# Reordering the first loads, touching rows ahead of them, and keeping a softmax in PSUM: a change to a fused attention and feed-forward kernel

## The chip, the cores and the metric

The kernel runs on one core of a Trainium2 chip. The metric is the device time of one execution in microseconds (us), lower is better. A quoted time is the median of several executions; a verdict needs a difference of 2%. Beside each timed execution stands the span that its profile shows; the time is 1.7 to 1.8 us longer than the span, so that spans of different kernels can be compared.

## The reference

The input `x` has 2048 rows of 512 values (bf16). It is normalized over each row; the result feeds two branches, and both are added to `x`.

```python
xn = layernorm(x)                                  # eps 1e-5, no weights
# A: 32 heads of 16; each position attends to 8 keys, at distances 0, 2, ..., 14
q, k, v = split(xn @ wqkv)                         # wqkv 512 x 1536
logits  = einsum("bhsd,bhswd->bhsw", q, kg) * 16 ** -0.5    # masked where the key would be before row 0
a = einsum("bhsw,bhswd->bhsd", softmax(logits), vg).reshape(...) @ wo
# B: gated feed-forward, 1376 wide
h = gelu(xn @ w_gate) * (xn @ w_up)
out = x + a + h @ w_down
```

## The kernel before

The program is laid out by a list scheduler inside the kernel file: every instruction is a task with an engine, an estimated duration, its reads and writes, and a priority (lower goes first); a table of shifts (`SHIFT`) moves the priorities of whole groups. The rows are worked on in four blocks of 512 (16 tiles of 128). After a short head, TensorE multiplies; the other engines evict, normalize, form the products for the attention (VectorE, the `UNI` tiles) and run the softmax. What the change and the argument touch:

```python
# loads, all on SyncE's queue, in the order of prio: x0 (two of 128 rows), Wq, x1, Wk, Wv, x2 ...
G.task("sp", "ld_x0_%d" % t2, 0, mk_ld(), wr=[(it_x, t2)], prio=-960 + t2, nbytes=128 * 1024)
XIN[:, it.slot, :, :], x2[256 * p:256 * p + 256, :].rearrange("(t q) d -> q t d", q=128))       # x1, x2, ...
G.task("sp", "ld_x%d" % p, ..., prio=(0, -899.5, -897.5, -897)[p] if p < 4 else -950 + p * 20)
Wqkv[:, :, i * 512:(i + 1) * 512], A_wqkv[:, i * 512:...].rearrange("(k p) n -> p k n", p=128)  # Wq, Wk, Wv
t_ld["w" + nm] = G.task("sp", "ld_w" + nm, 0, mk(), ..., prio=-900 + i, nbytes=512 * 1024)
# ... (cut)
# normalization of a tile: statistics, aggregate, + eps, square root on GpSimd (pow), reciprocal, (x - mean) * rstd
G.task("pool", "sq%d" % t, 0.65, ...)              # e.tensor_tensor(..., op=ALU.pow)
chain(["bnst0", "bnag0", "ve0", "bnst1", "rstd0", "norm0", "bnag1", "ve1", "sub1", "rstd1", "norm1",
       "bnst2", "bnag2", "ve2", "sub2", "bnst3", "rstd2", "norm2", "bnag3", "ve3", "sub3", "rstd3", "norm3"])
# ... (cut)
# softmax of a block: logits in two PSUM banks, differences, exponentials and sum in SBUF (tile DE)
out=dev(), in0=lgv(...), in1=msb(0), op=ALU.subtract          # d2: PSUM -> DE
e.activation(out=DE[...], in_=DE[...], func=ACTF.Exp)         # exp
e.tensor_reduce(out=msv(1), in_=devw(), axis=AX.X, op=ALU.add)# d4: sum over 8 keys
# ... (cut)
cparts = [(0, 256), (256, 512)] if t in TAIL_SPLIT else [(0, 512)]      # last two tiles of the output in halves
```

Of the kernel before, what the change touches and what calls it, by code (L numbers as in the profile page):

```python
# [16 lines left out]
    PE_SLACK=0.0,  # L17
# [90 lines left out]
class Task:  # L108
    def __init__(self, idx, eng, name, dur, emit, prio, table, nbytes, batch, mode=None, latest=None,
# [5 lines left out]
        self.urgent = False  # L115
        self.idx = idx
# [28 lines left out]
class Graph:  # L145
# [399 lines left out]
    def emit_engine(self, eng_name, e):  # L545
        for t in self.order[eng_name]:
            for (s, v) in t.waits:
                e.wait_ge(s, v)
            ins = t.emit(e)
            ins.then_inc(t.sem, 16 if eng_name == "sp" else 1)  # L550
            t.ins_name = ins.ins.name
        if eng_name == "sp":
            for (s, tot) in self.dma_totals:
                e.wait_ge(s, tot)
# [48 lines left out]
    def report(self):  # L603
# [14 lines left out]
    "acc0": 555, "acc1": 267, "acc2": -116, "acc3": -521, "fin1": -54, "h0": 161, "h1": 209, "h3": -1408,  # L618
    "ldb2": 112, "ln1": 18, "ln2": -227, "prod1": 166, "prod3": -74, "pv0": 110, "pv3": 290, "pvr1": 83,
    "pvr2": -911, "pvr3": 185, "qkv0": -19, "qkv2": -3186, "sm0": 543, "sm1": -535, "sm3": 287,  # L620
}
SCHED = dict(PE_SLACK=1.0, DMA_BPUS=250e3,
             TOL=dict(pe=1.0, act=-0.3, dve=0.3, pool=-0.3, sp=0.0))
# [32 lines left out]
def bass_parallel_sum__sliding_local_dilated__glu_gated_geglu__prompt_kernel(nc, A_x, A_wqkv, A_wo, B_x, B_w_gate, B_w_up, B_w_down, out, dbg=None, cfg=None):  # L656
    cfg = dict(cfg or {})
    NXIN = cfg.get("NXIN", 4)
    NSUBA = cfg.get("NSUBA", 1)
# [6 lines left out]
    NMS = cfg.get("NMS", 2)  # L666
    NDE = cfg.get("NDE", 1)
# [3 lines left out]
    NBS = cfg.get("NBS", 3)  # L671
# [4 lines left out]
    NOB = cfg.get("NOB", 2)  # L676
# [7 lines left out]
    TAIL_SPLIT = cfg.get("TAIL_SPLIT", [14, 15])  # L684
# [13 lines left out]
    with contextlib.ExitStack() as es:  # L698
        block = es.enter_context(nc.Block())

        def sb(name, shape, dt):
# [18 lines left out]
        wsrc = sb("wsrc", [128, 512], BF)  # L720
        onef = sb("onef", [128, 2], F32)
# [3 lines left out]
        mhalf = sb("mhalf", [128, 2], F32)  # L725
        ve = sb("ve", [128, NT], F32)
# [5 lines left out]
        DE = sb("DE", [128, NDE, 1024], F32)  # L732
# [28 lines left out]
        P_de = Pool("de", NDE)  # L761
# [28 lines left out]
        I_mhalf = Item("mhalf")  # L790
        I_ve = Item("ve")
# [8 lines left out]
        G.task("pool", "c_wsrc", 0.8, lambda e: e.memset(wsrc[:, :], 0.0), wr=[I_wsrc], prio=PC - 1)  # L800
# [6 lines left out]
               rd=[I_cf], wr=[I_ident], prio=PC)  # L807
        G.task("pool", "c_mhalf", 0.1, lambda e: e.memset(mhalf[:, :], 0.5), wr=[I_mhalf], prio=PC)
# [14 lines left out]
        G.task("pool", "c_wdz", 0.3, lambda e: e.memset(Wd[0:32, 10, :], 0.0), wr=[(I_wd, 2)], prio=PC2 + 20)  # L823
        G.task("pool", "c_htz", 0.3, lambda e: e.memset(HT[0:32, :, 10, :], 0.0), wr=[I_htz], prio=PC2 + 20)
# [12 lines left out]
            out=onef[:, 1:2], in_=onef[:, 0:1], func=ACTF.Gelu_apprx_tanh),  # L837
            rd=[(I_onef, 0)], wr=[(I_onef, 1)], prio=PC, table="gelu")
# [16 lines left out]

        t_ld = {}
        for i, nm in enumerate(("q", "k", "v")):
# [4 lines left out]
            t_ld["w" + nm] = G.task("sp", "ld_w" + nm, 0, mk(), wr=[(I_wq, nm)], prio=-900 + i, nbytes=512 * 1024)  # L862
# [33 lines left out]
        for p in range(NP):  # L896
# [5 lines left out]
            if p == 0:  # L902
                for t2 in range(2):
                    def mk_ld(t2=t2, it=it_x):
                        return lambda e: e.dma_start(XIN[:, it.slot, t2, :], x2[128 * t2:128 * t2 + 128, :])  # L905
                    G.task("sp", "ld_x0_%d" % t2, 0, mk_ld(), wr=[(it_x, t2)], prio=-960 + t2, nbytes=128 * 1024)
            else:
                def mk_ld(p=p, it=it_x):
                    return lambda e: e.dma_start(  # L909
                        XIN[:, it.slot, :, :], x2[256 * p:256 * p + 256, :].rearrange("(t q) d -> q t d", q=128))  # L910
                G.task("sp", "ld_x%d" % p, 0, mk_ld(), wr=[(it_x, 0), (it_x, 1)], prio=(0, -899.5, -897.5, -897)[p] if p < 4 else -950 + p * 20,
                       nbytes=256 * 1024)
# [13 lines left out]
            for ts in (((2 * p,), (2 * p + 1,)) if b == 0 else ((2 * p, 2 * p + 1),)):  # L926
# [3 lines left out]
                def mk_ve(t=t, n=n):  # L930
                    return lambda e: e.tensor_scalar(  # L931
                        out=ve[:, t:t + n], in0=mv[:, t:t + n, 1], scalar1=1e-5, scalar2=None, op0=ALU.add)
                t_of["ve%d" % t] = G.task("dve", "ve%d" % t, 0.09, mk_ve(), rd=[(I_mv, q) for q in ts],
                                          wr=[(I_ve, q) for q in ts], prio=pr + 1)

                def mk_sq(t=t, n=n):
                    return lambda e: e.tensor_tensor(  # L937
                        out=sq[:, t:t + n], in0=ve[:, t:t + n], in1=mhalf[:, 0:n], op=ALU.pow)
                t_of["sq%d" % t] = G.task("pool", "sq%d" % t, 0.65, mk_sq(), rd=[(I_ve, q) for q in ts] + [I_mhalf],
                                          wr=[(I_sq, q) for q in ts], prio=pr + 3)  # L940
# [549 lines left out]
```

## Time and profile before

| | before |
|---|---|
| time, median of 3 | 197.95 us (197.94 to 198.12) |
| profiled span | 196.6 us (of an execution that took 198.39) |
| TensorE busy | 188.7 us, 96% |
| VectorE / ScalarE / GpSimd busy | 153.6 / 103.6 / 21.4 us |
| first product with Wq / with Wk | 6.73 / 8.90 us after the start |
| fourth transpose (last input of block 0 ready) | 12.70 us |
| last matmul ends | 194.08 us |

To read it: TensorE has nearly nothing to give after 17.5 us, so a change that removes no matmul can gain in the head (where TensorE waits for loads and for the first normalizations), in the tail after the last matmul, and in what pauses the middle may have. One mark serves through the whole document: the start of the long series of V products after the 64 small products of block 0. It tells how long the head took. Where the trace lacks the first V product, the mark is taken from its weight load, which is there. In the kernel before it is 17.37, less the 0.87 us of a V group that ran earlier there: 16.50.

### The profile page before, as it was taken

The numbers are of one execution on the slowest core, as the hardware profiler recorded it, in microseconds if no ns is written. First come the engines' busy times: TensorE is split into PE (matmuls) and PEld (weight loads), VectorE is DVE, ScalarE is ACT, GpSimd is POOL, SyncE is SP. The second block draws the span as 40 slices with busy tenths as digits, with TensorE's granted clock in tenths as the row PEclk, the third lists the DMA queues.
The fourth block names the chain that finished last, engine by engine and source line by source line (L and its number), as shares of the span: only waits on it lengthen the run. The fifth ranks groups of instructions, "written<-read, shape, count | busy, mean of one in ns | idle before, by whom it ended". The sixth has DMA issues, their size and how long they took to land.

```text
span 196.6 us, 3169 instructions
## 1 busy us (share of the span) xinstructions
PE 188.7 (96%) x1189; PEld 90.6 (46%) x1208; DVE 153.6 (78%) x238; ACT 103.6 (53%) x167; POOL 21.4 (11%) x37
## 2 busy tenths in 40 slices
PE   7689999999999999999999999999999999999994
PEld 2486444444444443444444444444444443444483
DVE  3788999999999399998999889988791897142131
ACT  4366673687787758701647930473894105766000
POOL 6834001020870100000000000000000000000000
PEclk9999999999999999999999999999999999999999
DMA  5999999894444678054538036248414260010121
GB/s 127 363 370 332 318 175 147 227 279 94 106 126 110 179 121 210 0 145 125 161 107 213 5 118 171 64 129 210 114 53 110 71 169 27 0 34 25 36 84 42
DMA packets 34639, 27.03 MB, mean 137 GB/s; under 512 B 10976, under 2 KB 33088, under 8 KB 34624
## 3 DMA queue, kind: packets, MB, share of 16 engines
q1 hardware_dynamic: 34624, 26.83, 52.9%
q8 instruction: 9, 0.15, 0.3%
q14 instruction: 6, 0.05, 0.1%
HBM read 19.99 MB, written 5.26 MB: 128 GB/s over the span
## 4 chain that ended last, share of the span: by engine, by line
PE 91%; DMA 4%; SPq 1%; DVE 1%; issue 1%; ACT 0%; DVEq 0%
PE PS L1326 35%; PE PS L1405 19%; PE PS L1084 18%; PE PS L1401 7%; PE PS L1168 4%; DMA XIN<-in_A_x_dram 4%; PE PS L1295 3%; PE PS L1040 2%; PE PS L1361 2%; PE PS L1161 1%; SPq L859 1%; SPq L905 0%; DVE st L920 0%; ACT UU L1343 0%; SPq L909 0%
## 5 line engine op out<-in xcount | busy, mean ns | idle before, releaser
L1405 PE MATMUL PS<-Wd,HT 128*128 128x512 bf16 (+1 forms) x197 | 41.3, 355 | 0.1
L1326 PE MATMUL PS<-xnT,Wu 128*128 128x512 bf16 x158 | 40.2, 379 | 0.1
L1326 PE MATMUL PS<-xnT,Wg 128*128 128x512 bf16 x153 | 39.6, 379 | 0.7 <-issue 0.3
L1274 DVE TENSOR_TENSOR UNI<-BS,PT 128x2048 bf16<-128x2048 bf16 x32 | 37.2, 1219 | 2.2 <-PE PS L1295 2.1
L1138 DVE TENSOR_TENSOR UNI<-QT,KT 128x2048 bf16<-128x2048 bf16 x32 | 37.3, 1216 | 0.9 <-ACT KT L1059 0.9
L1336 ACT ACTIVATE GG<-PS 128x512 bf16<-128x512 f32 x40 | 24.0, 600 | 23.7 <-PE PS L1326 23.7
L1084 PE MATMUL PS<-xnT,Wqkv 128*128 128x512 bf16 x157 | 35.9, 379 | 0.3 <-issue 0.2
L1343 ACT ACTIVATE UU<-PS 128x512 bf16<-128x512 f32 x40 | 23.9, 601 | 7.7 <-PE PS L1326 7.7
L1405 PEld LDWEIGHTS PS<-Wd,HT 128*128 128x128 bf16 x198 | 19.4, 98 | 18.7
L1348 DVE TENSOR_TENSOR HT<-GG,UU 128x512 bf16<-128x512 bf16 x40 | 15.8, 415 | 12.4 <-ACT UU L1343 11.8
L1326 PEld LDWEIGHTS PS<-xnT,Wg 128*128 128x128 bf16 x160 | 15.3, 98 | 19.8 <-ACT UU L1343 0.8
L1326 PEld LDWEIGHTS PS<-xnT,Wu 128*128 128x128 bf16 x160 | 15.5, 98 | 19.2 <-ACT GG L1336 0.4
L1084 PEld LDWEIGHTS PS<-xnT,Wqkv 128*128 128x128 bf16 x160 | 15.4, 98 | 18.8 <-issue 0.4
L1425 DVE TENSOR_TENSOR OB<-PS,XR 128x512 bf16<-128x512 f32 (+1 forms) x18 | 11.3, 630 | 15.5 <-PE PS L1405 15.4
L1108 ACT ACTIVATE VT<-PS 128x512 bf16<-128x512 f32 x16 | 9.5, 596 | 13.7 <-PE PS L1084 13.7
L1401 PE MATMUL PS<-Wo,OT 128*128 128x512 bf16 (+1 forms) x67 | 16.2, 354 | 0.2
L1306 ACT ACTIVATE OT<-PS 128x512 bf16<-128x512 f32 x16 | 8.7, 595 | 13.2 <-PE PS L1295 13.2
L920 DVE BATCH_NORM_STATS2 st<-XIN 128x6 f32<-128x512 bf16 x16 | 10.8, 685 | 3.8 <-DMA XIN<-in_A_x_dram 3.8
L937 POOL TENSOR_TENSOR sq<-ve,mhalf 128x2 bf16<-128x2 f32 (+1 forms) x10 | 6.6, 662 | 34.7 <-DVE ve L931 34.7
L1401 PEld LDWEIGHTS PS<-Wo,OT 128*128 128x128 bf16 x72 | 7.1, 98 | 7.0
L1124 POOL COPY KT<-KT 128x64 bf16<-128x64 bf16 x3 | 9.4, 3118 | 7.7 <-ACT KT L1101 6.0
L1094 ACT ACTIVATE QT<-PS 128x512 bf16<-128x512 f32 x12 | 7.1, 595 | 4.8 <-PE PS L1084 4.8
(62 smaller groups left out, 142.8 us busy)
## 6 DMA issues: line engine op xcount, KB each, us to landing
BS<-vt_scratch SPq DMA_DIRECT2D x64, 128.5 KB, 3.0
vt_scratch<-VT SPq DMA_DIRECT2D x16, 128.0 KB
XR<-in_A_x_dram SPq DMA_DIRECT2D x16, 128.0 KB, 2.1
XIN<-in_A_x_dram SPq DMA_DIRECT2D x7, 256.0 KB, 7.2
out_dram<-OB SPq DMA_DIRECT2D x14, 128.0 KB, 1.9
Wqkv<-in_A_wqkv_dram SPq DMA_DIRECT2D x3, 512.0 KB, 6.6
Wg<-in_B_w_gate_dram SPq DMA_DIRECT2D x1, 1280.0 KB
Wu<-in_B_w_up_dram SPq DMA_DIRECT2D x1, 1280.0 KB
```

What stands on the lines that cost most here:

```text
L920: return lambda e: e.bn_stats(out=st[:, t, :], in_=XIN[:, it.slot, t2, :])
L1084: ins = e.matmul(PS[:, 512 * it.slot:512 * it.slot + HWD], lhsT=lhsT, rhs=xnT[:, itx.slot, kt, c0:c0 + HWD], start=(kt == 0), stop=(kt == 3))
L1108: return lambda e: e.activation(out=VT[:, ito.slot, 0:HWD], in_=PS[:, 512 * it.slot:512 * it.slot + HWD], func=ACTF.Identity)
L1138: return lambda e: e.tensor_tensor(out=UNI[:, it.slot, :, :], in0=bass.AP(QT, (itq.slot * 4 + g) * 512, [[NQT * 4 * 512, 128], [0, 4], [1, ...
L1274: return lambda e: e.tensor_tensor(out=bass.AP(UNI, ito.slot * 2048, [[NUNI * 2048, 128], [512, 4], [128, 4], [1, 128]]), in0=bass.AP(BS, ...
L1326: ins = e.matmul(PS[0:M, 512 * it.slot:512 * it.slot + 512], lhsT=Wx[:, kt, j * 128:j * 128 + M], rhs=xnT[:, itx.slot, kt, :], start=(kt = ...
L1336: return lambda e: e.activation(out=GG[0:M, ito.slot, :], in_=PS[0:M, 512 * it.slot:512 * it.slot + 512], func=ACTF.Gelu_apprx_tanh)
L1343: return lambda e: e.activation(out=UU[0:M, ito.slot, :], in_=PS[0:M, 512 * it.slot:512 * it.slot + 512], func=ACTF.Identity)
L1348: return lambda e: e.tensor_tensor(out=HT[0:M, ito.slot, j, :], in0=GG[0:M, ig.slot, :], in1=UU[0:M, iu.slot, :], op=ALU.mult)
L1401: ins = e.matmul(PS[:, 512 * it.slot:512 * it.slot + CW], lhsT=OT[:, ito.slot, dq, ti * 128:(ti + 1) * 128], rhs=Wo[:, dq, c0:c1], start=( ...
L1405: ins = e.matmul(PS[:, 512 * it.slot:512 * it.slot + CW], lhsT=HT[:, ith.slot, j, ti * 128:(ti + 1) * 128], rhs=Wd[:, j, c0:c1], start=Fal ...
L1425: return lambda e: e.tensor_tensor(out=OB[:, ito.slot, 0:CW], in0=PS[:, 512 * it.slot:512 * it.slot + CW], in1=XR[:, itx.slot, c0:c1], op= ...
```

## The change

Its intent: bring the first weights sooner and smooth the start of the queue (two tiny reads across `wqkv` and `x` on ScalarE's queue ahead of everything; x0, Wq, Wk, x1 in place of x0, Wq, x1, Wk); shorten the first normalizations (roots on ScalarE instead of GpSimd, fills on VectorE, statistics of tile 4 after tile 3's normalization); take work off VectorE (softmax in PSUM, without the `DE` tile); and re-tune the priorities for it. The diff, cut to its core:

```diff
-    "acc0": 555, "acc1": 267, "acc2": -116, "acc3": -521, "fin1": -54, "h0": 161, ...
+    "acc0": 47, "acc1": -436, "acc3": 127, "er0": -106, "er1": 318, "er2": 764, ...      (all of SHIFT is new)
-SCHED = dict(PE_SLACK=1.0, ..., TOL=dict(pe=1.0, act=-0.3, dve=0.3, pool=-0.3, sp=0.0))
+SCHED = dict(PE_SLACK=1.6, ..., TOL=dict(pe=0.6, act=-0.3, dve=-0.3, pool=-0.3, sp=0.0))
-    NSUBA 1; NMS 2; NDE 1; NBS 3; NOB 2
+    NSUBA 0; NSQA 2; NMS 1; NBS 4; NOB 3
-        G.task("pool", "c_wsrc", ...)  "c_wdz", "c_htz" on "pool"
+        G.task("dve", "c_wsrc", ...)   "c_wdz", "c_htz" on "dve"
-            out=onef[:, 1:2], in_=onef[:, 0:1], func=ACTF.Gelu_apprx_tanh),
+            out=onef[:, 1:2], in_=onef[:, 0:1], func=ACTF.Sqrt),
+        for i, (src, n, stride) in enumerate(((A_wqkv, 64, 8 * 1536), (A_x, 12, 32 * 512))[:cfg.get("NTCH", 2)]):
+            def mk(src=src, n=n, stride=stride, i=i):
+                return lambda e: e.dma_start(tch[0:n, 32 * i:32 * i + 32],
+                                             bass.AP(src.tensor, i * 128 * 512, [[stride, n], [1, 32]]))
+            t_w = G.task("sp", "touch%d" % i, 0.01, mk(), wr=[(I_tch, i)], prio=-970 + i, nbytes=64)
+            t_w.on_act = True
-            t_ld["w" + nm] = G.task("sp", "ld_w" + nm, 0, mk(), wr=[(I_wq, nm)], prio=-900 + i, ...)
+            t_w = G.task("sp", "ld_w" + nm, 0, mk(), wr=[(I_wq, nm)], prio=(-958, -957.5, -898)[i], ...)
-                ... prio=(0, -899.5, -897.5, -897)[p] if p < 4 else -950 + p * 20
+                ... prio=(0, -957, -897.5, -897)[p] if p < 4 else -950 + p * 20
+                if t < NSQA:
+                    t_of["sq%d" % t] = G.task("act", "sq%d" % t, 0.15, mk_sa(), ...)   # Sqrt(var + eps) on ScalarE
-        chain(["bnst0", "bnag0", "ve0", "bnst1", "rstd0", "norm0", "bnag1", "ve1", "sub1", ..., "norm3"])
+        chain(["bnst0", "bnag0", "sub0", "rstd0", "norm0", "bnst1", "bnag1", "sub1", ..., "norm3", "bnst4"])
+        chain(["norm3", "bnst5"])
-                    out=dev(), in0=lgv(...), in1=msb(0), op=ALU.subtract)
+                    out=lgv(...), in0=lgv(...), in1=msb(0), op=ALU.subtract)
-   exp: out=DE, in_=DE      sum: in_=devw()      multiply: in0=dev()
+   exp: out=lgv, in_=lgv    sum: in_=lgv(...)    multiply: in0=lgv(...)
-    TAIL_SPLIT: tiles 14, 15: [(0, 256), (256, 512)]
+    TAIL_SPLIT: 14: [(0, 256), (256, 512)], 15: [(0, 256), (256, 384), (384, 512)]
```

## The prediction

> **What bounds the kernel now.** I read the page's busy table first, then busy time by stretch, then the timeline of the first 18 us, and last the tail.
>
> ```profile
> PE 188.7 (96%) x1189; PEld 90.6 (46%) x1208; DVE 153.6 (78%) x238; ACT 103.6 (53%) x167; POOL 21.4 (11%) x37
> ...
> 0.00:17.50 17.50, 13.58 (x158) 9.81 (x160) 12.41 (x43) 8.94 (x15) 9.21 (x30) 1.00 0.92 302
> 17.50:194.00 176.50, 175.02 (x1033) 80.78 (x1048) 140.73 (x194) 94.67 (x152) 12.18 (x7) 1.00 0.50 123
> 194.00:196.60 2.60, 0.07 (x1) 0.00 (x0) 0.42 (x1) 0.00 (x0) 0.00 (x0) 0.90 0.14 40
> ```
>
> First the page's share of busy time, then three stretches (columns: PE, weight loads, VectorE, ScalarE, GpSimd busy, granted clock, DMA share, GB/s). From 17.5 to 194 us TensorE is busy 175.02 of 176.50 us at clock 1.00, and nothing in the change removes a matmul there. So the middle can give at most 1.48 us. What is left is a head of 17.5 us and a tail of 2.6 us. The head is where TensorE really waits:
>
> ```profile
> 5.46 0.40 PE L992 MATMUL PS<-ident,XIN 128*128 128x128 bf16 x4 [0.22 <-DVE XIN L964]
> ...
> 6.73 1.05 PE L1040 MATMUL PS<-xnT,Wqkv 128*128 128x128 bf16 x16 [0.66 <-DMA Wqkv<-in_A_wqkv_dram]
> ...
> 8.90 1.96 PE L1040 MATMUL PS<-xnT,Wqkv 128*128 128x128 bf16 x32 [0.90 <-DMA Wqkv<-in_A_wqkv_dram]
> 9.08 0.94 POOL L824 MEMSET HT<- 32x1024 bf16 x1
> ...
> 9.42 0.75 DVE L967 TENSOR_SCALAR XIN<-XIN,rstd 128x512 bf16<-128x512 bf16 x1
> ...
> 11.08 0.70 DVE L920 BATCH_NORM_STATS2 st<-XIN 128x6 f32<-128x512 bf16 x1 [0.38 <-DMA XIN<-in_A_x_dram]
> ...
> 12.70 0.40 PE L992 MATMUL PS<-ident,XIN 128*128 128x128 bf16 x4 [0.72 <-DVE XIN L967]
> ```
>
> The timeline (start, duration, what it waited for before): the first product with Wq starts at 6.73 on the arrival of Wq, the first with Wk at 8.90 on the arrival of Wk, and the fourth transpose at 12.70 on a normalization that stood behind a statistics instruction of tile 4, which itself waited for its load until 11.08. After 12.70 the 64 remaining small products and 4 V matmuls run without a hole to 17.53.
>
> ```profile
> 2.50:3.00 0.50, 0.50 (x2) 0.15 (x1) 0.02 (x1) 0.00 (x0) 0.37 (x3) 1.00 0.91 246
> 3.00:3.50 0.50, 0.50 (x3) 0.16 (x2) 0.50 (x1) 0.00 (x0) 0.22 (x1) 1.00 1.35 113
> 3.50:4.00 0.50, 0.50 (x3) 0.22 (x2) 0.43 (x4) 0.08 (x1) 0.00 (x0) 1.00 0.29 82
> 4.00:4.50 0.50, 0.50 (x3) 0.22 (x2) 0.50 (x2) 0.50 (x1) 0.34 (x1) 1.00 0.79 231
> 4.50:5.00 0.50, 0.50 (x3) 0.00 (x0) 0.34 (x2) 0.14 (x1) 0.50 (x4) 1.00 1.02 350
> ```
>
> In these half-microseconds the last column falls from 246 to 113 and 82 GB/s, then climbs to 350: a dent of about 0.74 us (two halves at about 97 instead of 370) plus 0.2 us in the next half, 0.9 us in all, just as the weights begin to be read.
>
> **What the Trainium skill says.** "DMA: Bandwidth & Descriptors", section "Why a DMA increments its semaphore by 16 and not by 1": a transfer runs on up to 16 engines that finish independently, and only the full count means that all has landed. The trace agrees in kind: by 6.73 us the half-microsecond rates add up to about 1.31 MB, while x tiles 0 and 1 and Wq are only 0.79 MB; some engine is far behind the others when Wq is counted as landed. Same page, "Issuing engines are not separate DMA queues": issuing from a second engine saves only issue time; the bytes share the 16 engines. Nothing in the trace of before issues from ScalarE, so no line tests it. "ScalarE: Activation LUTs", section "What ACT_TABLE_LOAD costs", gives 1283 ns a load; the trace has 9 loads of 1283 ns each. "VectorE: DVE Perf Modes", section "Why PSUM operands drop a tier": fp32 from PSUM runs at the base rate. The softmax's 128x1024 fp32 instructions take 1222 ns out of PSUM and 1213 ns out of SBUF, so PSUM costs VectorE nothing.
>
> **The change part by part.**
>
> *Touches.* Two tiny reads on ScalarE's queue across Wqkv and the first 384 rows of x. Their intent is plainly to take whatever makes the dent before the real reads come. If they do, up to 0.9 us of dent goes, and engines that fall in step again bring Wq and Wk forward by more. They are the first two things ScalarE does; at the 0.4 us that an issue takes on SyncE, plus a 1.28 us table load and the 0.20 us dummy, ScalarE is free at about 3.1 us (estimate), before the first root is wanted at 3.9.
>
> *Order of loads.* x0, x0, Wq, x1, Wk becomes x0, x0, Wq, Wk, x1. Wk gains 0.26 MB of queue, 0.7 us at 360 GB/s; x1 loses 0.52 MB, 1.5 us. Without the touches x1 would land at 7.36 + 1.5 = 8.9. With them I put Wq at about 5.5, Wk at 6.5 to 7.2 and x1 at 6.8 to 7.9.
>
> *Roots on ScalarE, subtraction on VectorE (tiles 0, 1).* Before: aggregate ends 3.89, add 0.15, power on GpSimd 0.57, reciprocal, normalization ends 5.40. After: root 0.2 beside a subtraction of 0.34, reciprocal 0.17, normalization 0.35: it ends at about 4.75. The transpose then waits for the 9 warm-up matmuls (9 x 0.43 = 3.86 us). Their zero fill goes to VectorE, 0.25 instead of 0.53, so they end at about 4.95 instead of 5.24. First transpose 5.0, first product 6.15 instead of 6.73.
>
> *Fills off GpSimd, chain reordered.* The 0.94 us fill on GpSimd ran beside the normalization that took 0.75 instead of 0.35; that overlap goes. Tile 4's statistics are put behind the normalization of tile 3, so a late load no longer holds it (the 11.08 line).
>
> *Sum for the head.* With x1 at 6.8: statistics 7.55, aggregate and add 7.9, power 8.5, normalization of tile 2 9.4; tile 3 the same way, done at 10.9. TensorE: products from 6.15, Wk products 7.6 to 9.7, transposes at 9.7 and 11.2, then 64 products of 0.0558 us (3.57 us by 13.09 to 17.53 less 0.87 of V) end at 15.2. Before, the same work without V ends at 17.53 - 0.87 = 16.7. Gain 1.5. With x1 at 7.9 normalization 3 ends at 12.05 and the gain is 0.6. With no effect of the touches (x1 at 8.9) it ends at 13.05 and the head loses 0.4. I expect 1.1.
>
> *Softmax in PSUM.* The sum over SBUF cost 1914 ns, the same reduction out of PSUM 1222: 4 x 0.69 = 2.8 us less VectorE work, none of it on the path. But the two banks of the logits stay taken until the last multiply: about 1.3 table load, 1.06 exponential, 1.22 sum, 0.94 reciprocal, 1.21 multiply, with other VectorE work between, so some 6 to 8 us longer in each of four blocks. Price put at 0 to 0.4 us; my expectation is 0.1.
>
> *One more table load.* The roots' set must give way to gelu's after the third V eviction: 1.28 us of ScalarE, with three gate matmul groups of 0.86 us to run before a bank is missed (3 x 0.86 = 2.6 against 1.3 + 0.6). At most 0.1 us.
>
> *New priorities, deeper BS and OB buffers.* The order of TensorE's work changes; following it by hand, block 1's logits come at 69 us and their eight products are done 3 us before. So I see neither a new wait nor much of the 1.48 us recovered: 0.3 gained.
>
> *Tail.* The last 256 columns are cut in two. 15 matmuls of 128 columns at 0.0558 are 0.84 us, twice that is 1.67; one 256 piece takes 1.64. Same TensorE time; the last add drops from 425 to about 290 ns and the last store halves. Gain about 0.15.
>
> Sum: -1.1 + 0.1 + 0.1 - 0.3 - 0.15 = -1.35, so 196.6 us.
>
> **The rivals.** (1) The touches do nothing, or delay x0 themselves: then x1 at 8.9 holds the head, and the time is 197.8 to 198.4. For it: x1 was moved back 1.5 us on purpose, and 64-byte reads are served by the same engines. Against: the dent in the rates is real and brief. (2) PSUM banks run short: the gate and up matmuls wait in each block, four times 0.5 us or more, 198 to 200. For it: eight banks, two pinned longer; against: ScalarE evicts in 0.6 us and TensorE fills in 0.86, so few banks suffice. (3) Everything fits and the new order also closes the small holes: 1.5 + 1.3 + 0.2, 195.0 us. Even then the gain stays under 2% (194.0), which would need the middle to be faster than TensorE's own work.
>
> **Range and chances.** Head from -1.5 to +0.4, middle from -1.0 to +1.0, tail -0.1 to -0.3: 8 in 10 between 195.3 and 197.9. Faster by over 2% needs 3.95 us, more than the head's and middle's sum: 0.03. Slower by over 2% needs rival 2 at full size: 0.03.
>
> **What would show it.** GB/s near 350 already at 3 to 4 us; the first Wq product at about 6.2, the first Wk product before 8; the last of the first four transposes near 11.2; V matmuls from about 15.2; TensorE busy over 98.5% from there to the end. Wrong if the dent stays, if TensorE shows waits on ScalarE or VectorE of half a microsecond after a logits group, or if the head gains and the end doesn't move by as much.

## The result

The changed kernel took 198.09 us (median of 4, 197.76 to 198.59) beside 198.03 us before (4 runs). Ratios in this document are the mean time of one kernel's fast runs over that of the other's of the same rounds, so they are not quite the ratio of the medians. Here it is 1.0003, with a 95% interval of 0.9979 to 1.0027: the same. The predicted 196.6 us and the range 195.3 to 197.9 were not met. In a second set of five rounds the changed kernel took 197.79 against 197.90 us, ratio 0.9999 [0.9983, 1.0014]. So a gain of 1.35 us (0.7%) is excluded; 0.3 us either way is not.

The page's line of busy times of the changed kernel, and below it busy time by stretch (columns: PE, weight loads, VectorE, ScalarE, GpSimd busy, granted clock, DMA share, GB/s), the counterparts of the first fence of the prediction:

```profile
PE 190.6 (97%) x1223; PEld 91.1 (46%) x1223; DVE 153.9 (78%) x241; ACT 104.1 (53%) x169; POOL 9.6 (5%) x33
```

```profile
0.00:17.50 17.50, 14.13 (x160) 10.16 (x161) 12.38 (x41) 8.81 (x17) 5.64 (x27) 1.00 0.93 310
17.50:194.00 176.50, 176.42 (x1065) 80.98 (x1063) 141.21 (x200) 95.30 (x153) 3.97 (x7) 1.00 0.51 122
194.00:196.40 2.40, 0.00 (x0) 0.00 (x0) 0.29 (x1) 0.00 (x0) 0.00 (x0) 1.00 0.12 27
```

Look at the counts. Here PE and its weight loads have 1223 records each. Before there were 1189 matmul records beside 1208 weight loads, although each matmul here has one weight load. Nineteen records of the kernel before were missing. In the stretch from 17.5 to 194 us the counts are 1033 against 1048 (weight loads run ahead of their products, so the edges of a stretch blur the difference), and the trace has 18 gaps on TensorE there, each at a place where the next product starts one 128x512 product (216 ns) late. They add up to the whole 1.48 us in which TensorE seemed idle in the middle before (0.08 us each, and not 0.216, since the records of neighbouring products overlap). In the changed kernel, with no record missing, TensorE is busy 176.42 of the same 176.50 us; in its second profiled execution, which has 1204 of its 1223 records, only 174.52. From the V mark to the first piece of tile 14's output (both by the timeline) the two kernels take the same time: 187.35 - 16.50 = 170.85 us before, 187.17 - 16.33 = 170.84 us after. The middle neither gained nor lost, because there was nothing to gain.

The head, from the timeline of the changed kernel (start, duration, what it waited for):

```profile
0.81 0.54 ACTq L873 DMA_DIRECT2D tch<-in_A_wqkv_dram  x1
1.38 0.79 ACTq L873 DMA_DIRECT2D tch<-in_A_x_dram  x1
...
4.42 0.38 DVE L1001 TENSOR_SCALAR XIN<-XIN,rstd 128x512 bf16<-128x512 bf16 x1
...
5.06 0.60 PE L1026 MATMUL PS<-ident,XIN 128*128 128x128 bf16 x4
...
6.55 1.05 PE L1076 MATMUL PS<-xnT,Wqkv 128*128 128x128 bf16 x16 [0.67 <-ACT sq L959]
...
7.86 1.96 PE L1076 MATMUL PS<-xnT,Wqkv 128*128 128x128 bf16 x32
...
8.51 0.69 DVE L945 BATCH_NORM_STATS2 st<-XIN 128x6 f32<-128x512 bf16 x1 [1.44 <-DMA XIN<-in_A_x_dram]
...
12.52 0.40 PE L1026 MATMUL PS<-ident,XIN 128*128 128x128 bf16 x4 [0.26 <-DVE XIN L1001]
12.75 3.74 PE L1076 MATMUL PS<-xnT,Wqkv 128*128 128x128 bf16 x64
```

The first normalization ends at 4.80, as planned, and the first transpose starts at 5.06 instead of 5.46. The first product with Wk no longer waits and comes at 7.86 instead of 8.90. But VectorE stands idle for 1.44 us until x1 has landed, and its statistics start at 8.51 instead of 7.36. The same line of the kernel before:

```profile
7.36 0.69 DVE L920 BATCH_NORM_STATS2 st<-XIN 128x6 f32<-128x512 bf16 x1 [0.41 <-DMA XIN<-in_A_x_dram]
```

From there to the fourth transpose it takes 12.52 - 8.51 = 4.01 us, and before it took 12.70 - 7.36 = 5.34. So x1 comes 1.15 us later and the chain of tiles 2 and 3 is 1.33 us shorter: the gain and the loss cancel, and the fourth transpose is only 0.18 us earlier than before. The V mark moves by 0.17 us, from 16.50 to 16.33.

The rates of the same half-microseconds as in the prediction:

```profile
3.00:3.50 0.50, 0.50 (x3) 0.22 (x2) 0.50 (x1) 0.49 (x2) 0.36 (x2) 1.00 0.77 54
3.50:4.00 0.50, 0.50 (x3) 0.15 (x2) 0.43 (x3) 0.34 (x2) 0.42 (x3) 1.00 0.70 213
4.00:4.50 0.50, 0.50 (x2) 0.15 (x1) 0.47 (x3) 0.16 (x1) 0.35 (x3) 1.00 1.00 324
```

54, 213 and 324 GB/s in place of 113, 82 and 231: the dent is there, somewhat shorter. The difference is (54 + 213 + 324 - 113 - 82 - 231) x 0.5 us = 0.08 MB, or 0.2 us at 370 GB/s.

In the tail TensorE takes the same time, as predicted: from the first piece of tile 14 to the last matmul (by the chain of waits) 193.93 - 187.33 = 6.60 us, and 194.08 - 187.52 = 6.56 before. The last addition takes 0.29 instead of 0.42 us. So the tail gained about 0.1 us.

### The profile page after: what moved, and what is told of

Read it like the earlier page. It is cut to its first block, busy times and chain, and to the rows that moved or that the text cites. A ratio compares the mean times of both kernels' runs of the same rounds, so it can differ in the third digit from the quotient of the medians.

```text
span 196.4 us, 3247 instructions
## 1 busy us (share of the span) xinstructions
PE 190.6 (97%) x1223; PEld 91.1 (46%) x1223; DVE 153.9 (78%) x241; ACT 104.1 (53%) x169; POOL 9.6 (5%) x33
## 4 chain that ended last, share of the span: by engine, by line
PE 92%; DMA 3%; DVE 2%; SPq 1%; POOL 0%; issue 0%; DVEq 0%
PE PS L1357 36%; PE PS L1436 19%; PE PS L1120 18%; PE PS L1432 7%; PE PS L1326 4%; PE PS L1204 4%; DMA XIN<-in_A_x_dram 3%; PE PS L1076 2%; PE PS L1392 2%; PE PS L1197 1%; DVE st L945 1%; SPq L881 0%; SPq L929 0%; DVE XIN L1001 0%; POOL sq L969 0%
## 5 line engine op out<-in xcount | busy, mean ns | idle before, releaser
L1436 PE MATMUL PS<-Wd,HT 128*128 128x512 bf16 (+2 forms) x209 | 41.3, 345 | 0.0
L1357 PE MATMUL PS<-xnT,Wg 128*128 128x512 bf16 x160 | 40.3, 379 | 0.0
L1456 DVE TENSOR_TENSOR OB<-PS,XR 128x512 bf16<-128x512 f32 (+2 forms) x19 | 11.5, 605 | 17.6 <-PE PS L1436 17.6
L1432 PE MATMUL PS<-Wo,OT 128*128 128x512 bf16 (+2 forms) x76 | 16.9, 345 | 0.0
L1137 ACT ACTIVATE KT<-PS 128x512 bf16<-128x512 f32 x12 | 7.2, 597 | 4.8 <-PE PS L1120 4.8
L969 POOL TENSOR_TENSOR sq<-ve,mhalf 128x2 bf16<-128x2 f32 (+1 forms) x8 | 5.5, 688 | 64.6 <-DVE ve L956 64.6
```

The lines of the kernel that those rows point to most:

```text
L1357: ins = e.matmul(PS[0:M, 512 * it.slot:512 * it.slot + 512], lhsT=Wx[:, kt, j * 128:j * 128 + M], rhs=xnT[:, itx.slot, kt, :], start=(kt = ...
L1432: ins = e.matmul(PS[:, 512 * it.slot:512 * it.slot + CW], lhsT=OT[:, ito.slot, dq, ti * 128:(ti + 1) * 128], rhs=Wo[:, dq, c0:c1], start=( ...
L1436: ins = e.matmul(PS[:, 512 * it.slot:512 * it.slot + CW], lhsT=HT[:, ith.slot, j, ti * 128:(ti + 1) * 128], rhs=Wd[:, j, c0:c1], start=Fal ...
L1456: return lambda e: e.tensor_tensor(out=OB[:, ito.slot, 0:CW], in0=PS[:, 512 * it.slot:512 * it.slot + CW], in1=XR[:, itx.slot, c0:c1], op= ...
```

## The experiments

Theory T after the result: the touches do next to nothing, and the new order of loads, which only pays if they work, takes back what early roots and the later statistics of tile 4 give. Rivals: the touches help but something else in the head eats it; the PSUM softmax or the new priorities cost in the middle what the head gains; the time is bound by something other than TensorE. "Mark" is the V mark explained above, each from one profiled execution. In eight of the profiled executions of the changed kernel and its variants (its own two and those of x1 before Wk, before Wq and before Wq with more warm-up, of no touches, and both of x1 before Wk without touches) it takes 177.58 or 177.59 us from the mark to the end of the last matmul, so that there the head alone sets the difference; in the one with roots on GpSimd it is 177.81, and in the kernel before 177.57. Two profiled executions of one kernel differ by up to 0.7 us in the mark.

| run | mark, us | time, us | ratio to before |
|---|---|---|---|
| before | 16.50 | 197.9 to 198.1 | |
| changed kernel | 16.33 | 198.09 | 1.0003 |
| changed kernel, again | 16.02 | 197.79 | 0.9999 |
| without touches | 16.44 | 197.78 | 0.9995 |
| x1 before Wk | 15.32 | 197.07 | 0.9954 |
| x1 before Wq | 17.43 (1.6 of it by the slow clock) | 197.79 | 0.9994 |
| x1 before Wq, more warm-up | 15.87 | 197.68 | 0.9978 |
| x1 before Wk, without touches | 15.94 and 15.22 | 196.59 and 196.92 | 0.9934 and 0.9944 |
| x1 before Wk, roots on GpSimd | 15.36 | 197.40 | 0.9965 |
| before, tile 4's statistics later | 15.27 | 197.61 | 0.9987 |
| before, Wk before x1 | 16.96 | 199.53 | 1.0087 |
| before, softmax in PSUM | 15.93 | 200.89 | 1.0155 |

**The changed kernel once more** (no edit).

> The changed kernel once more, unedited, as the yardstick for this chip. Both theories: 197.7 to 198.6 us, ratio 0.998 to 1.002, tile 2's statistics start at 8.3 to 8.7 us (arrival of x1), the first V matmul at 16.2 to 16.5 us.

Measured 197.79 us (197.57 to 198.38, 6 runs), ratio 0.9999 [0.9983, 1.0014]; x1's statistics at 8.19. The result is no accident of one set of runs.

**Without the touches.**

```diff
-        ...((A_wqkv, 64, 8 * 1536), (A_x, 12, 32 * 512))[:cfg.get("NTCH", 2)]):
+        ...((A_wqkv, 64, 8 * 1536), (A_x, 12, 32 * 512))[:cfg.get("NTCH", 0)]):
```

> The changed kernel without the two touches. Theory T (the touches hardly move the transfers): tile 2's statistics start at most 0.3 us later than in after_again, first V matmul at 16.3 to 16.7, the dent in the GB/s at 3 to 4.5 us nearly as in the kernel before, time within 0.3 us of after_again. Rival R1 (the touches do save the 0.9 us that the prediction gave them, and the new load order eats it): statistics at 9.2 to 9.5, V at 17.0 to 17.4, time 0.6 to 0.9 us longer.

Measured 197.78 us (197.53 to 198.22), ratio 0.9995 [0.9981, 1.0010]. x1's statistics start at 8.61 without touches, and at 8.51 and 8.19 in the two profiled executions with them: 0.1 to 0.4 us; the mark is 16.44 against 16.33 and 16.02. That is no more than two executions of one kernel differ (0.7 us in the mark, below). As many bytes as x0 and Wq have (0.79 MB) have arrived by 5.2 us in both profiled executions of the changed kernel, and by 5.0 to 5.4 us in seven profiles without touches. The end does not move. The touches are worth nothing that can be measured.

**x1 before Wk again** (the old order of loads in the changed kernel).

```diff
-                         prio=(-958, -957.5, -898)[i], nbytes=512 * 1024)
+                         prio=(-958, -956.5, -898)[i], nbytes=512 * 1024)
```

> The changed kernel with its loads in the old order (x1 ahead of Wk). Theory T (the head is held by x1's arrival, through tile 3's normalization): tile 2's statistics start at about 7.1, Wk arrives at about 8.5, the fourth transpose at about 12.2 instead of 12.5, the first V matmul at 15.8 to 16.1 instead of 16.3, time 0.2 to 0.5 us shorter. Rival R2 (the arrival of Wk holds the head): V at 16.7 to 17.0, time 0.4 to 0.7 us longer.

Measured 197.07 us (196.76 to 197.18), ratio 0.9954 [0.9941, 0.9968]. Its timeline:

```profile
7.16 0.69 DVE L945 BATCH_NORM_STATS2 st<-XIN 128x6 f32<-128x512 bf16 x1
...
8.60 1.96 PE L1076 MATMUL PS<-xnT,Wqkv 128*128 128x128 bf16 x32 [0.74 <-DMA Wqkv<-in_A_wqkv_dram]
...
11.52 0.39 PE L1026 MATMUL PS<-ident,XIN 128*128 128x128 bf16 x4
11.74 3.74 PE L1076 MATMUL PS<-xnT,Wqkv 128*128 128x128 bf16 x64
```

TensorE now waits 0.74 us for Wk, yet the fourth transpose no longer waits for anything and comes 1.0 us sooner than in the changed kernel's first profile (I had expected 12.2). The mark moves by 1.0 us against that profile (16.33 to 15.32), by 0.7 against the second (16.02), and the time by 0.7 (medians of the same rounds) to 0.9 (0.0045 x 198). The gain in the head reaches the end, and the order of loads alone ate it. It was more than I expected (0.2 to 0.5). With x1 there by 7.16, the arrival of Wk (8.60) holds the head here.

**x1 even before Wq.**

```diff
-                             prio=(0, -957, -897.5, -897)[p] if p < 4 else ...
+                             prio=(0, -958.5, -897.5, -897)[p] if p < 4 else ...
```

> The changed kernel with x1 ahead of Wq and Wk. Theory T: tile 2's statistics no longer wait for a load, Wq arrives at about 7.1 and Wk at 8.5; the matmuls then run without a hole from there, V at 15.7 to 16.0, time 0.3 to 0.6 us shorter. Rival R2: V at 16.7 or later. The dent: if it belongs to the first reads of Wqkv, the GB/s stays high until about 4 us and dips after; if it belongs to the time since the start, it dips at 3.0 to 4.0 us as before, under x1.

Measured 197.79 us, but with a wide range (197.04 to 199.26). Two of six executions took 199.25 us at a mean clock of 0.991, the profiled one among them; the other four took 197.04 to 198.18 at 1.000. The profiled one, timeline and then busy time by microsecond:

```profile
7.77 1.05 PE L1076 MATMUL PS<-xnT,Wqkv 128*128 128x128 bf16 x16 [1.82 <-DMA Wqkv<-in_A_wqkv_dram]
...
9.14 3.53 PE L1076 MATMUL PS<-xnT,Wqkv 128*128 128x128 bf16 x32
```

```profile
8.00:9.00 1.00, 1.00 (x19) 0.88 (x16) 1.00 (x4) 0.00 (x0) 0.61 (x1) 1.00 1.10 384
9.00:10.00 1.00, 0.91 (x10) 0.87 (x10) 0.89 (x5) 0.91 (x2) 0.22 (x1) 0.53 1.14 331
10.00:11.00 1.00, 1.00 (x12) 1.00 (x11) 0.52 (x2) 0.17 (x1) 0.38 (x1) 0.50 1.10 237
```

Wq now comes behind x1, TensorE stands idle for 1.82 us, and some time after that the granted clock falls to one half for about 3.4 us (0.53, 0.50, 0.50 and 0.76 on average in the four microseconds from 9): 32 products take 3.53 us instead of 1.96. That is a price of leaving a hole, beside the hole itself. Wq was used at 7.77 where I had expected 7.1, and V did not start at 15.7 to 16.0. As to the dent, the rates in slices of 0.15 us from 3.0 to 4.2 us are 116 to 218 GB/s, under x1's load with Wq's still behind it. By the expectation that spoke for the time or the place in the queue, and against the first reads of `wqkv`; the looks below come back to it. The Trainium skill, "TensorE: Matmul & The Clock Gate", section "Part 1: The HAM clock gate (the 'warmup' mystery)", has the two states, half and full speed, and a free-running window of about 3.4 us by which they are chosen. The half speed and its length agree here.

**The same with the hole filled** by seven more warm-up matmuls.

```diff
-        WARM = cfg.get("WARM", (9, 1))
+        WARM = cfg.get("WARM", (9, 8))
```

> The kernel with x1 loaded before Wq (197.79 us, where the products with Wq came after a hole of 1.82 us and 32 of them took 3.53 us instead of 1.96) with 8 instead of 1 warm-up matmuls in that hole. Theory T: the slow products come from TensorE having stood idle; with the hole filled to about 8.5 us the 32 products take about 2.0 us, granted clock 1.0 in the head, fourth transpose near 12.5 instead of 13.6, time 196.5 to 197.2. Rival: the slow products wait on something else (late packets of Wq): still 3 us or more for 32, time 197.6 to 198.0.

Measured 197.68 us (197.26 to 198.40), ratio 0.9978 [0.9959, 0.9998]. The 32 products take 1.95 us again, and the clock is 1.0 (0.999 in one) in all six executions: the slow products came from TensorE's idleness. Two in six against none in six is thin by itself, but the other traces say the same: each hole on TensorE of 1.8 us or more that any of them shows is followed by slow products (1.82 us here, 1.98 in the run with fewer matmuls, 2.23, 2.36, 5.16, 3.04 and 2.03 in the looks; in all but the last the clock record shows one half for 3.4 us or more), and no hole of up to 1.64 us is. In executions without a trace the holes are unknown. The time misses my 196.5 to 197.2, because it fell only where the drop had happened; the four undisturbed executions before were at 197.5 on average already. As an order of loads, x1 ahead of Wq has no advantage.

**x1 before Wk, without touches** (both edits above).

> a2_x1_before_wk without the touches. Theory T (load order is what counts, touches are worth at most a few tenths in the head and nothing measurable at the end): fourth transpose at 11.4 to 11.9 us, Wk products at 8.5 to 9.0, time within 0.3 us of a2 (ratio to before 0.994 to 0.998). Rival R1 (touches carry part of a2's gain): fourth transpose at 12.2 or later, ratio above 0.998.

Measured 196.59 us (196.42 to 197.65, 7 runs), ratio 0.9934 [0.9916, 0.9953]. The theory's figures were missed: the fourth transpose came at 12.14 and Wk's products at 9.23 in the profiled execution (one of the slower ones, 197.65), and the time is 0.48 us below that of x1 before Wk with touches, where at most 0.3 was expected. By its ratio the rival (touches carry part of the gain) is out.

> The same kernel as the run with x1 before Wk and no touches (196.59 us, ratio 0.9934). Theory T: it is a property of the kernel: again 196.4 to 196.9, ratio 0.992 to 0.995, fourth transpose near 12.1. Rival: half of it was that run's luck: 197.0 to 197.3, as with the touches.

Measured 196.92 us (196.78 to 197.39, 6 runs), ratio 0.9944 [0.9928, 0.9960]: the ratio is within what was expected, the time at its edge; the fourth transpose came at 11.42, not near 12.1. Over both sets this version is 0.6% or 1.2 us faster than the kernel before, and so than the changed kernel, whose ratio is 1.000. It is the best that was found, and it has no touches; its intervals overlap that of the version with touches. Its two profiled executions show how much the head of one kernel varies: mark 15.94 (Wq waited for 1.39 us, that execution took 197.65) and 15.22 (0.79 us, 196.95).

**Roots back on GpSimd**, in the version with x1 before Wk and with touches.

```diff
-    NSQA = cfg.get("NSQA", 2)
+    NSQA = cfg.get("NSQA", 0)
```

> The changed kernel with x1 loaded before Wk (as the run that took 197.07 us) and, besides, the roots of tiles 0 and 1 back on GpSimd. Theory T: early roots are hidden, because TensorE waits for Wq until about 6.6 us either way; the first transpose comes about 0.4 us later (5.4 instead of 5.06), the first Wq product at most 0.2 us later, the fourth transpose stays within 0.3 us of 11.5, time 196.9 to 197.4. Rival: they are worth what they save in the chain (the prediction's 0.65 us for the first normalization), then 197.6 to 197.8. The re-laid middle can move either by 0.3 us, or more if it meets a hole, which the profile would show.

Measured 197.40 us, ratio 0.9965 [0.9951, 0.9980], against 0.9954 with the roots on ScalarE. The first transpose comes at 5.36 instead of 5.06, the fourth at 11.55 instead of 11.52. The early roots do what they were meant to, and it buys nothing on TensorE. The first product with Wq starts at 6.46 with the roots on GpSimd and at 6.57 with them on ScalarE, where Wq came that much later, and in both TensorE then waits for Wk (to 8.53 and 8.60).

**Only the later statistics of tile 4**, in the kernel before.

```diff
-               "norm3"])
+               "norm3", "bnst4"])
+        chain(["norm3", "bnst5"])
```

> The kernel before with one thing of the change alone: the statistics of tiles 4 and 5 stand behind the normalization of tile 3. Theory T (the hole before the fourth transpose came from that order, and it is the part of the change that gains): fourth transpose at 11.6 to 12.0 instead of 12.7, time 0.5 to 1.0 us shorter than before, ratio 0.995 to 0.998. Rival R3 (the fourth transpose was held by the power on GpSimd and by x1 anyway, or the matmuls that follow wait for something else): fourth transpose above 12.3 and ratio 0.999 to 1.001.

Measured 197.61 us, ratio 0.9987 [0.9970, 1.0004]. The fourth transpose comes at 11.48 instead of 12.70 and the mark moves 1.23 us. Of that, 0.44 us is x1, which landed earlier in this execution (its statistics start at 6.92 instead of 7.36, with the same loads). The chain from there to the fourth transpose takes 4.56 us instead of 5.34, or 5.13 in the profile of the softmax run below, whose head is the same: this one line gives 0.6 to 0.8 us of the head. But only 0.3 us arrived. The scheduler lays the middle out anew from changed estimates, with priorities that were tuned for the old layout. From the chain of waits of this run:

```profile
141.41 0.60 ACT GG L1370
142.01 0.50 ACT GG L1337
...
142.55 6.22 PE PS L1327 x28
```

TensorE waits there for two evictions by ScalarE, which the kernel before does not show at that place. Its profiled span is 0.7 us shorter than before for a head that is 1.23 us shorter; the middle gave 0.5 us back (178.04 us from the mark to the end of the last matmul, 177.57 before).

**Only the new order of loads**, in the kernel before.

```diff
-  ... prio=(0, -899.5, -897.5, -897)[p] if p < 4 else -950 + p * 20
+  ... prio=(0, -898.5, -897.5, -897)[p] if p < 4 else -950 + p * 20
```

> The kernel before with nothing but the new order of loads (x0, Wq, Wk, x1). Theory T (the order is what ate the head's gain): x1's statistics at 8.5 to 8.9 instead of 7.36, Wk product at 7.9 instead of 8.9, fourth transpose near 13.7 to 14.2 instead of 12.7, time 198.6 to 199.2. Rival: the order is neutral (Wk's gain pays for x1's loss, the gap lies elsewhere): 197.7 to 198.2. The scheduler re-lays the middle slightly.

Measured 199.53 us (199.10 to 201.31), ratio 1.0087 [1.0054, 1.0119]; one of the six executions, 201.31, had the clock drop (0.991). x1's statistics at 8.29, Wk's first product at 8.12, the fourth transpose at 13.16, the mark 0.46 us later than in the profile of before, and 1.0 us later than in that of the softmax run below with the same head: in the head less than expected, in the time more. The order costs, as theory T says, though about a third of the loss (0.45 of 1.4 us) comes from the middle, which has the same two evictions at 143 us in its chain. The order of loads is worth 0.7 to 1.0 us in the changed kernel and 0.5 to 1.0 us in the head of the kernel before.

**Only the softmax in PSUM**, in the kernel before (the softmax part of the diff above, with the old priorities and buffers).

> The kernel before with the softmax in PSUM and nothing else (the scheduler re-lays the middle). Theory T (VectorE is off the path): VectorE busy falls by 2.5 to 3.0 us, TensorE's middle stays packed, ratio 0.998 to 1.002. Rival R4 (two banks held longer starve the matmuls): waits of TensorE on ScalarE or VectorE after the logits, 0.5 us a block, ratio above 1.004.

Measured 200.89 us (200.56 to 201.66), ratio 1.0155 [1.0133, 1.0177]: 3 us slower, where 0.998 to 1.002 was expected; the rival R4 has the direction. VectorE's busy time fell to 150.7 us, the 2.9 us that was worked out. The chain of waits of this run:

```profile
137.16 1.28 ACT L1213
...
138.45 1.01 ACT PS L1213
...
139.98 1.28 ACT L1331
...
141.28 0.61 ACT GG L1331
...
182.29 0.61 ACT UU L1338
...
182.92 0.44 DVE HT L1343
```

From 137 to 142 us the end of the kernel hangs on ScalarE. It loads the exponential's table (1.28), works 1.01 us on the logits in PSUM, loads gelu's table (1.28), and only then evicts the gate products for which TensorE needs the bank. With two of eight banks pinned by the logits, TensorE has less to go on with meanwhile: it is busy 19.11 of 20 us between 140 and 160. Some 1.7 us are lost at 139 to 142 us. A second hole, of 1.15 us at 182.3 to 183.4, follows the two last lines: an eviction by ScalarE and VectorE's product behind it. The Trainium skill, "PSUM — Partial Sum Buffer", section "Summary: rules for kernel authors", says "Evacuate promptly — 2 MiB is tight"; this run puts 3 us on it, of which about 0.5 us may be the anew laid-out middle that also the last two kernels paid for. In the changed kernel TensorE is busy 176.42 of 176.50 us with the same softmax. So something else in the change covers the price in full, most likely the new priorities (and perhaps the deeper buffers). That is an inference: the new priorities were not run alone in the kernel before, nor the changed kernel with its softmax in SBUF. Taken alone, the PSUM part is a loss.

**Fewer matmuls, a wrong result**, in the changed kernel: four of the eleven products with `w_down` are left out in all output groups of a block but the first.

```diff
-                            for j in js:
+                            for j in (js if len(js) < NJ else js[4:]):
```

> The changed kernel with four matmuls left out of each output group but the first of a block, order and waits as they were; wrong result on purpose. 40 matmuls of 512 columns at 0.2157 us, 12 of 256 at 0.109 and 8 of 128 at 0.056: 8.6 + 1.3 + 0.4 = 10.4 us of TensorE time. Theory T (from the head on TensorE is the only bound): the time falls by 9.5 to 10.4 us. Rival R5 (VectorE or ScalarE is just behind TensorE in the middle): it falls by less than 8 us and TensorE shows holes.

Measured 190.90 us (2 runs), ratio 0.9645 [0.9610, 0.9680]: 7.0 us less instead of 10.4 (7.5 less in the execution at full clock; in the other it fell to a mean of 0.991). TensorE bounds the middle, but some 3 us behind it stands the next limit, and with 10.4 us taken out holes open: what R5 had said (less than 8 us, and holes). In the profiled execution, the slower one, the clock fell after a hole of 1.98 us at 118.3 us. From the chain:

```profile
116.93 3.12 DMA xnT<-XIN
...
156.32 2.61 DMA PT<-pt_scratch
...
163.75 5.69 DVE UNI L1305 x5
```

They are the transposing loads of the next block (behind a row of other issues on SyncE), the loads of the softmax's result, and VectorE's products.

**What the dent is.** The touches were meant for the dent in the rates at 3 to 4 us, and they leave it. Five more looks ask to what it belongs. Each line below is the rate in forty slices of 0.15 us from the start to 6 us. First the version with x1 before Wk and no touches:

```profile
GB/s 0 0 0 0 0 0 0 0 0 0 0 0 82 130 307 314 219 205 307 191 143 116 177 48 48 116 239 321 328 396 369 396 355 355 348 376 355 362 355 362
```

x0's bytes arrive from 1.8 us on at 200 to 300 GB/s; Wq's begin at about 2.85 us with 48 to 191 GB/s and need until 4.05 to reach 320.

Wq first of all (its priority -962 instead of -958):

> The best version (x1 before Wk, no touches) with Wq's load first in the queue, ahead of x0. A look at the rates in slices of 0.15 us, not at the time (x0 comes later, so the head must get longer, by about 1 us). Theory A (first reads of Wqkv's addresses) and F (form of the load): the dent moves to the front: the first 1 us of bytes (from 1.8 us) stays under 200 GB/s, and no dent at 3 to 4 us. Theory P (time, or third place): Wq starts at over 300 GB/s and the dent under 120 GB/s stands at 2.7 to 3.9 us as before.

```profile
GB/s 0 0 0 0 0 0 0 0 0 0 0 0 14 48 48 184 123 34 68 205 253 321 362 403 375 403 376 403 355 396 369 383 321 341 341 376 341 321 300 314
```

The slow stretch moved to the front, 1.8 to 2.85 us, and from 3.15 us on all is fast. So it is bound neither to the time nor to the third place in the queue (theory P is out), and here it comes with Wq's load.

x1 first of all (priority -962 instead of -957):

> The same with x1's load (the form with two rows for each partition) first in the queue, then x0, then Wq. Theory A: x1 starts at full rate, the dent comes when Wq begins (3 to 4 us). Theory F: the slow start is at x1, from 1.8 us on, and Wq, which has the same form, starts without one. Theory P: the dent stands at 2.7 to 3.9 us, whatever is read then.

```profile
GB/s 0 0 0 0 0 0 0 0 0 0 0 0 41 177 266 164 123 300 369 382 362 294 150 150 116 68 61 143 137 171 130 191 232 266 239 307 355 348 376 314
```

x1, with two rows for each partition, has a shallow dip at 2.3 us; a deep one comes from 3.3 to 4.8 us. Whose bytes those are is not shown: at 3.3 us only 0.37 of the 0.52 MB of x1 and x0 had passed, and x0's second half landed only after 3.97 us. (This run took 217 us: its middle was laid out badly, with VectorE's products on the chain. It is not used for time.)

A dense touch, 64 bytes of each of the 512 rows of `wqkv`, in the changed kernel with x1 before Wk:

```diff
+                if i == 0:
+                    return lambda e: e.dma_start(
+                        tchd[:, :, :], bass.AP(src.tensor, 0, [[1536, 128], [128 * 1536, 4], [1, 32]]))
```

> The changed kernel with x1 before Wk, its touch of Wqkv made dense: 64 bytes of each of the 512 rows in place of each eighth row. Theory A (and the touches were merely too thin): the dent goes, rates over 250 GB/s from 3.0 us on, x1's statistics near 6.5 instead of 7.2. Theories F and P: the dent stays, under 150 GB/s somewhere in 2.7 to 3.9 us, and 512 more packets may make it worse.

```profile
GB/s 0 0 0 0 0 0 0 0 0 0 0 0 184 205 172 249 206 198 329 365 153 55 7 27 89 75 109 280 239 300 355 348 335 335 314 307 369 362 403 369
```

7 to 109 GB/s from 3.15 to 4.05 us: the dent is deeper than ever. Thinness of the touches in rows was not their fault. This touch itself reads four rows for each partition, 64 bytes of each, and its 512 packets had all moved by 3.1 us, before the dent.

Wq in four loads of 128 rows, the form of x0's:

```diff
+                for k4 in range(4):
+                        return lambda e: e.dma_start(Wqkv[:, k4, 0:512], A_wqkv[128 * k4:128 * k4 + 128, 0:512])
```

> The best version with Wq's load in four loads of 128 rows, the form of x0's two loads. The issues cost about 1.3 us more on SyncE, so x1 and Wk come later; a look at the rates only. Theory F (form): no slice of 0.15 us under 150 GB/s between 2.7 and 4 us, since four such loads stream as x0's two do (over 200 GB/s). Theory A (first reading of these bytes): still slices under 120 GB/s there.

```profile
GB/s 0 0 0 0 0 0 0 0 0 0 0 0 177 246 246 280 225 219 280 205 239 259 321 164 253 273 232 314 362 205 225 219 219 225 150 212 321 375 355 253
```

No dent at 3 to 4 us. The rates are those that one issue of 128 KB in each 0.5 us or so allows, about 260 GB/s. The bytes first read from `wqkv` are the same, so it is not their first reading as such. In this run the rate falls to 168 GB/s between 6.0 and 6.5 us, where 1.06 MB have passed and Wk, now the first load of Wq's form, begins.

The whole of Wq read twice, once ahead of everything (into the place that Wg takes later):

```diff
+        G.task("sp", "ld_wdummy", 0, lambda e: e.dma_start(Wg[:, :, 0:512],
+            A_wqkv[:, 0:512].rearrange("(k p) n -> p k n", p=128)), wr=[I_wg], prio=-963, nbytes=512 * 1024)
```

> The best version with one more load of the whole of Wq ahead of everything, into the place that Wg takes later. The head gets longer by 1.4 us or more; a look at the rates only. Theory A: the slow start is at the front, and when Wq is read the second time (after x0, about 3.9 us and later) there is no dent: all slices over 200 GB/s from 3.2 us on. Theory F: a dent at each of the two, the second as deep as the first (some slices under 150 GB/s between 3.5 and 5 us).

```profile
GB/s 0 0 0 0 0 0 0 0 0 0 0 0 20 82 20 41 116 157 89 116 177 239 375 375 369 403 369 416 348 417 348 410 328 396 335 376 341 375 362 376
```

A slow start at the front, and none when the same load comes the second time. Neither theory covers both looks: four small loads have no dent at 3 to 4 us, so the form of the load seems to matter, but only the first load of that form pays (the second Wq has none, nor has Wk where it follows Wq). My best guess is a start-up cost of about 0.8 us for the first large load with several rows for each partition, wherever it stands. It is not shown. Each look is one execution; the dense touch has four rows for each partition and did not take the dent away, so the guess needs whole rows, or SyncE's queue, to count; and with x1 ahead of Wq (above) the dip stands under x1's two rows. What makes the dent up, below the level of the rates, stays open, and so does whether a touch of whole rows would take it. Splitting Wq brings no time that one run can show (197.21 us, mark 15.34, between the two marks of the version it was made from): Wq and x1 land about 0.5 us earlier (by 5.76 and 6.49 us, against 6.26 and 6.97), but Wk's first product comes at 8.63.

## Why the prediction was wrong

By the terms of its sum (-1.1 head, +0.1 softmax banks, +0.1 table load, -0.3 middle, -0.15 tail):

- **Touches: the step that failed.** "If they do, up to 0.9 us of dent goes, and engines that fall in step again bring Wq and Wk forward by more." The dent stayed (54 GB/s at 3.0 to 3.5 us) and the engines did not fall in step: the 16 counts of Wq's semaphore came over 1.26 us after and 1.28 before (and over 0.55 to 0.84 us in other executions, with and without touches alike). Worth 0.1 to 0.4 us in the head at most, and 0.0 at the end when taken out. The text had called their purpose "plainly" given. That was an intent read off the code; no line of the profile supported it, and not even a touch of every row took the dent away.
- **Order of loads: with that, a loss.** x1 was put at 6.8 to 7.9 "with them"; it was used at 8.51 (8.19 in the second profile). The alternative in the same paragraph, 8.9 without touches, was close (8.61 measured). In the changed kernel x1 holds the chain that sets the end of the head, and Wk, which gained, does not. Put back, the time falls by 0.7 to 0.9 us.
- **The working of the head was right otherwise.** Given x1's true time, its steps hold: from x1's use to the end of tile 3's normalization it allowed 4.1 us, and the changed kernel takes 3.95 (8.51 to 12.46). That the version with the old order gains 1.2 us, as much as the 1.1 predicted for the head, is partly luck: there the arrival of Wk at 8.5 to 8.6 sets the head, which the prediction did not foresee. What it lists as "chain reordered" is the largest gain (0.6 to 0.8 us by the statistics of tile 4 alone; 1.33 for the whole chain, in which the normalization of tile 2 also no longer runs beside the GpSimd fill). So the measured near zero is that gain against the late x1. The early roots buy nothing (0.3 us at the first transpose, 0.03 at the fourth).
- **Middle, -0.3: there was nothing to recover.** "So the middle can give at most 1.48 us" rests on busy time with matmul records missing: the 1.48 us are 18 gaps, each at the place of one missing product. The counts that give it away (x1033 beside x1048) stood in the quoted lines.
- **Softmax in PSUM, +0.1: right only inside the whole change.** As the price of the two banks it is wrong by a factor of some 20 to 30: 3.0 us with the old priorities, and rival 2 (198 to 200 us) described that kernel. In the changed kernel something covers it, most likely the new priorities (not tested alone); the prediction credited them with a gain instead.
- **Table load and tail: right.** Gelu's table load at 19.73 to 21.0 us opens no hole on TensorE; the tail gained about 0.1 us, with the same time on TensorE.

What remains is -0.17 for the head, 0 for the middle and about -0.1 for the tail: some 0.3 us, which the profiled spans show as 0.2 (196.6 and 196.4) and the timed runs can't tell from zero. In essence rival 1 happened, "the touches do nothing"; its 197.8 to 198.4 us holds the measured 198.09. I had weighed it by how real the dent was, not by whether a touch acts on it.

## What to carry to other kernels

When a change reorders loads, ask which load stands on the chain that ends last, not which one somebody waits for: moving the waited-for Wk ahead of x1 removed a visible wait of 0.9 us and cost 0.7 to 1.0 us in the head. Compare the counts of matmuls and weight loads before calling a rest of a per cent idle time. And test a part of a tuned change alone before crediting it: the same PSUM softmax costs 3 us in one kernel and nothing that shows in another.

## What the Trainium skill lacked or had wrong

- "DMA: Bandwidth & Descriptors" has no cost for the first large load with several rows for each partition. Here about 0.8 us go by at under 200 GB/s near the start of the queue: at Wq where Wq is first of all, not at four loads of 128 rows in its place, not at a second load of the same form; 64 bytes of each row read before it don't take it away. What causes it stays open (single executions).
- "TensorE: Matmul & The Clock Gate" asks for no idle gaps over some 3 us between bursts. Here one hole of 1.82 us was enough, and none of up to 1.64 us was: the mean clock was 0.991 in two of six executions of one kernel (199.25 against 197.04 to 198.18 us; in the profiled one of the two it was at one half for about 3.4 us), and 0.999 or 1.0 in all six with the hole filled.
- "PSUM — Partial Sum Buffer" gives no figure for holding banks: two of eight held over a softmax cost up to 3.0 us (ratio 1.0155, in two holes of TensorE), and nothing that shows in the changed kernel, whose order of work was tuned with it.
- "Perfetto Trace Analysis" does not say that a trace can lack matmul records (1189 of 1208 here) and that the missing ones look like idle time (18 gaps, 1.48 us).
